# An output projection contracted in tiles of 128 rows, its last 64 rows holding high and low parts in one tile

## The chip, the cores and the metric

The kernel runs on one core of a Trainium2 chip. The metric is the device time of one execution in microseconds; before the change the median of three runs is 2657.58 (2653.82 to 2659.47). The profile is one further execution, taken by the hardware profiler. TensorE (PE) multiplies matrices and loads its stationary operand with separate instructions (PEld); VectorE (DVE), ScalarE (ACT) and GpSimd (POOL) do elementwise work; SyncE (SP) issues all DMAs from one queue.

## The reference

Input x has 2048 tokens of width 576, layer normalized without weights to xn. Attention with 32 heads of width 18 and a gated feed-forward of width 4608 both read xn, and the second gates the first:

```python
qkv = (xn @ wqkv).reshape(B, S, 3, H, Dh).transpose(2, 0, 3, 1, 4)
scores = einsum("bhqd,bhkd->bhqk", q, k) * (Dh ** -0.5)
o = einsum("bhqk,bhkd->bhqd", softmax(scores), v)
s = o.transpose(0, 2, 1, 3).reshape(B, S, D) @ wo
g = silu((gelu(xn @ w_gate) * (xn @ w_up)) @ w_down)
return x + s * g
```

The change concerns the product with wo: 2048 x 576 by 576 x 576.

## The kernel before

All large products but that of the values run in fp32r, a format of fewer bits than fp32. To keep the accuracy a factor is split into a high part, rounded to fp32r, and a low part, the rest; a product then has three terms, high by high, high by low and low by high. `split` (L93) does that on POOL with two instructions, one for each part.

The tokens are cut into four blocks of 512 (`TB`). A prologue (L138 to L349) normalizes x, computes queries, keys and values, and stores them with the split x and the split wo (`split_wo`, `store_wo`, L281 to L291; scratch `wos`) in DRAM. Then comes a row of sections, one for each 128 columns of the gate and up weights and block of tokens, 144 in all. The first nine run ahead of the attention; then 128 sections carry a quarter of a unit of attention each (a unit is four heads by one block of tokens); seven follow it. In a section TensorE does 27 pairs of gate and up products (pg and pu, L369, 64 rows each, one in the upper and one in the lower half of the array) with, between them, products for scores (pe, L684) and for their maxima (pm, L653); then the values (acc, L718, 32 products), then possibly one group of the output projection (po, L550), and in every second section the down projection (py, L406, 48 products of 128 rows and 288 columns; in the last sections 24 in each). TensorE's order is that of the program. On the other engines and in SP's queue a scheduler places instructions in the order of the times it expects, save those kept in program order.

The output projection works on `OT`, which holds the transposed attention output of a block. Each unit of attention stores its four heads, unnormalized, to DRAM (`oT`), and the reciprocals of its sums to `rT`. `load_o` (L493) brings a tile of `OT` back, and spreads the reciprocals of each head over its 18 rows (tile `den`); `norm_o` (L504) multiplies the two on POOL. A tile holds 7 heads, 126 rows (`HO`, `KO`), so that the 576 rows take four tiles of 126 and one of 72 (`NK` = 5). `load_wo` (L508) loads half the columns (288) of wo's high and low part, in two transfers each. `split_o` (L516) splits 128 tokens of all five tiles at once into `oh` and `ol`. `project_o` (L540) does one group: 128 tokens by 288 columns, 3 terms for each of 5 tiles, 15 products into one PSUM bank; eight groups a block, 32 in all.

When these happen is written in a list of due sections, `at(n, part, ...)` (L566), with three parts: 0 ahead of the values, 1 ahead of the down projection, 2 behind it. The loop at L574 fills it. A tile of `OT` is loaded when its last head is done, and normalized two sections later; the groups of a block follow in every second section of the next block. In the last block the heads of the last unit are only done at the end of the attention: its last tile is loaded right behind (L814) and normalized first thing (L801). Six of its groups then stand in the sections that follow, the last two behind all other products (L825 to L852), where VectorE combines them with the gate and SP stores the result.

Of the kernel before, what the change touches and what calls it, by code (L numbers as in the profile page):

```python
# [8 lines left out]
F32 = mybir.dt.float32  # L9
F32R = mybir.dt.float32r  # L10
AF = mybir.ActivationFunctionType
ALU = mybir.AluOpType
# [4 lines left out]
S, D, H, DH, F = 2048, 576, 32, 18, 4608  # L17
P = 128
NT = S // P
TB = 512  # L20
NB = S // TB
KT = 4
R0 = KT * P
HR = 64
# [3 lines left out]
QD = 4  # L28
VW = QD * (DH + 1)
NQ = H // QD  # L30
NU = NQ * NB
NS = 2 * NT
SLOTS = 8
NA = NS // SLOTS
# [6 lines left out]
FIRST = (0, 0, 5, 5, 6, 6, 6, 6, 6)  # L41
ATT = range(len(FIRST), len(FIRST) + NU * NA)
MROW = 3 * DH
HO = 7
KO = HO * DH
NK = -(-D // KO)
EPS = 1e-5
GC = 0.044715
GS = 0.7978845608028654
# [3 lines left out]
def f(ap):  # L53
    return ap.bitcast(F32)
# [13 lines left out]
def kernel(ctx: ExitStack, tc: tile.TileContext, x, wqkv, wo, w_gate, w_up, w_down, out):  # L68
    nc = tc.nc
    x = x.rearrange("b s d -> (b s) d")  # L70
# [9 lines left out]
    oT = dram.tile([NQ, P, S], F32, name="oT")  # L80
    wos = dram.tile([2, D, D], F32, name="wos")
# [11 lines left out]
    def split(hi, lo, raw):  # L93
        first = nc.gpsimd.tensor_scalar(hi, raw, 1.0, 1.0, op0=ALU.mult, op1=ALU.mult)  # L94
        nc.gpsimd.tensor_tensor(lo, raw, f(hi), op=ALU.subtract)  # L95
        return first
# [9 lines left out]
    def raw_tile(shape, pool=wts):  # L106
        return pool.tile(shape, F32, name="raw", tag="raw", bufs=2)
# [30 lines left out]
    with tc.tile_pool(name="pro", bufs=1) as pro, tc.tile_pool(name="pps", bufs=1, space=PSUM) as pps:  # L138
# [140 lines left out]
            nc.sync.dma_start(vs[t * P:(t + 1) * P, c * H // 2:(c + 1) * H // 2, :], v)  # L279

        def split_wo(k):  # L281
            n = min(KO, D - k * KO)
            raw = raw_tile([KO, D])
            tc.keep_in_program_order(nc.sync.dma_start(raw[0:n], wo[k * KO:k * KO + n, :]))
            hi, lo = (pro.tile([KO, D], F32R, name=f"wo{i}", tag="rawp", bufs=5) for i in range(2))
            split(hi[0:n], lo[0:n], raw[0:n])
            return k, n, hi, lo

        def store_wo(k, n, hi, lo):
            for i, t in enumerate((hi, lo)):  # L290
                tc.keep_in_program_order(nc.sync.dma_start(wos[i, k * KO:k * KO + n, :], f(t)[0:n]))  # L291

        NQT = 2 * D // P
        def after(what, before):
# [191 lines left out]


    op = ctx.enter_context(tc.tile_pool(name="op", bufs=1, reuse_waits="tile"))
    OT = op.tile([KO, NK, TB], F32, name="OT")
    nc.gpsimd.memset(OT, 0.0)  # L490
    OW, OG = {}, {}

    def load_o(b, k, pool=op):  # L493

        h0, h1 = k * HO, min(H, (k + 1) * HO)
        n = (h1 - h0) * DH
        toks = slice(b * TB, (b + 1) * TB)
        den = pool.tile([KO, TB], F32, name="den")
        nc.sync.dma_start(OT[0:n, k, :], oT.rearrange("g (a p) t -> (g a) p t", p=32)[h0:h1, 1:DH + 1, toks])
        nc.sync.dma_start(den[0:n], rT[h0:h1, toks].rearrange("h (o s) -> h o s", o=1)  # L500
                          .to_broadcast([h1 - h0, DH, TB]))
        OG["den", k] = n, den

    def norm_o(k):  # L504
        n, den = OG.pop(("den", k))
        nc.gpsimd.tensor_tensor(OT[0:n, k, :], OT[0:n, k, :], den[0:n], op=ALU.mult)

    def load_wo(c):  # L508
        for i, name in enumerate(("woh", "wol")):
            w = OW[i] = op.tile([KO, NK, 288], F32R, name=name)  # L510
            cc = slice(288 * c, 288 * c + 288)
            m = (NK - 1) * KO
            nc.sync.dma_start(f(w)[:, 0:NK - 1, :], wos[i, 0:m, cc].rearrange("(k p) n -> p k n", p=KO))
            nc.sync.dma_start(f(w)[0:D - m, NK - 1, :], wos[i, m:D, cc])

    def split_o(i, pool=op):  # L516

        j = i % (TB // P)
        oh, ol = (pool.tile([KO, NK, P], F32R, name=m) for m in ("oh", "ol"))
        split(oh, ol, OT[:, :, j * P:(j + 1) * P])  # L520
        OG["o"] = oh, ol

    def place(b, i):
# [15 lines left out]

    def project_o(b, i, S2=None, o=None):  # L540
        c, j = divmod(i, TB // P)
        cc = place(b, i)[1]
        if b < NB - 1:
            xx, yy = OG["xy"]
        po = ps.tile([P, TB], F32, name="po", tag="m", bufs=3)
        o = o or OG["o"]
        terms = [(k, x, w) for k in range(NK) for x, w in ((0, 0), (0, 1), (1, 0))]
        for m, (k, x, w) in enumerate(terms):
            n = min(KO, D - k * KO)
            nc.tensor.matmul(po[:, 0:288], o[x][0:n, k, :], OW[w][0:n, k, :], start=(m == 0), stop=(m == len(terms) - 1))  # L550
        if b < NB - 1:
            nc.vector.scalar_tensor_tensor(yy, yy, 0.25, po[:, 0:288], op0=ALU.mult, op1=ALU.mult)
            nc.gpsimd.tensor_tensor(yy, yy, xx, op=ALU.add)
            OG["y", b, i] = yy
        elif S2 is not None:
            nc.scalar.activation(S2[:, j, cc], po[:, 0:288], AF.Copy)
        return po[:, 0:288]
# [8 lines left out]
    def at(n, part, what, *args):  # L566
        todo.setdefault((n, part), []).append(lambda: what(*args))
# [3 lines left out]
            t()  # L571

    S2 = [None]
    for b in range(NB):  # L574
        last = b == NB - 1
        for k in range(NK):
            t0 = b * AB + max(-(-min(H, (k + 1) * HO) // QD) * NA + 3, 22 + 3 * k)
            if not (last and k == NK - 1):
                at(t0, 0, load_o, b, k)
                at(t0 + 2 - last, 2, norm_o, k)  # L580
        first = (b + 1) * AB + 1 if last else max((b + 1) * AB + 6, (b + 1) * NR * G - len(FIRST) + 3)
        if not last:
            first += (first + len(FIRST)) % G
        at(first - 2, 0, load_wo, 0)
        at(first - 1, 2, split_o, 0)
        for i in range(GROUPS):
            n = first + i * (1 if last else G)
            if last and n >= ENDS - 1:
                continue
            if not last:  # L590
                at(n, 0, load_xy, b, i)
                at(n + 1, 0, store_y, b, i)
            at(n, 1, lambda b=b, i=i: project_o(b, i, S2[0]))
            if i == TB // P - 1:
                at(n + 1, 0, load_wo, 1)
            if i + 1 < GROUPS:
                at(n, 2, split_o, i + 1)
# [199 lines left out]
    with tc.tile_pool(name="epi", bufs=1, reuse_waits="tile") as epi:  # L797
        S2[0] = epi.tile([P, TB // P, D], F32, name="S2")
        XX = epi.tile([P, TB // P, D], F32, name="XX")
        n = NU * NA  # L800
        todo[n, 2].insert(0, lambda: norm_o(NK - 1))  # L801
        def cut(hi, lo, raw):
            split_av(hi, lo, raw, tc.keep_in_program_order)

        def early(raw):
            wd = [epi.tile([P, G, D], F32R, name=m, bufs=2) for m in ("dh", "dl")]
            cut(*wd, raw)
            return wd

        while FF["n"] < NF:  # L810
            section([], "m" if n % 2 else "f", (lambda: raw_tile([P, G, D], epi)) if n > NU * NA + 1 else None,
                    early if n == ENDS - 1 else None)
            if n == NU * NA:
                load_o(NB - 1, NK - 1, epi)  # L814
            if n == NU * NA + 3:
                tc.keep_in_program_order(nc.sync.dma_start(XX, x[S - TB:S, :].rearrange("(j p) d -> p j d", p=P)))
            tasks(n, 0)
            downs()
            tasks(n, 1)
            tasks(n, 2)  # L820
            finish(epi, cut, 2)
            n += 1
        assert not todo
        HIND = ENDS - 1 - (NU * NA + 1)
        project_o(NB - 1, HIND, S2[0])  # L825
        os = []
        for i in range(HIND + 1, GROUPS):
            split_o(i, op if i == HIND + 1 else epi)
            os.append(OG.pop("o"))
        downs()  # L830

        def put(ss, j, cc, add):
            rows = slice(S - TB + j * P, S - TB + (j + 1) * P)
            add.tensor_tensor(ss, ss, XX[:, j, cc], op=ALU.add)
            nc.sync.dma_start(out[rows, cc], ss)

        late = {}
        for Y, j, c in finals:
            cc = slice(288 * c, 288 * c + 288)
            th = epi.tile([P, 288], F32, name="thl", bufs=len(finals))  # L840
            ss = S2[0][:, j, cc]
            gate(th, th, Y[:, j, cc])
            if c * (TB // P) + j > HIND:
                late[c * (TB // P) + j] = th, ss, j, cc
            else:
                nc.vector.scalar_tensor_tensor(ss, th, 0.25, ss, op0=ALU.mult, op1=ALU.mult)
                put(ss, j, cc, nc.gpsimd)
        for i, o in zip(range(HIND + 1, GROUPS), os):
            th, ss, j, cc = late[i]
            po = project_o(NB - 1, i, o=o)  # L850
            nc.vector.scalar_tensor_tensor(ss, th, 0.25, po, op0=ALU.mult, op1=ALU.mult)
            put(ss, j, cc, nc.vector)  # L852
# [28 lines left out]
```

## Time and profile before

| what | value |
| --- | --- |
| median of the runs | 2657.58 us |
| profiled execution, its own time | 2655.82 us |
| its span, first to last instruction | 2654.0 us |
| mean granted clock of TensorE | 0.999 |
| attention sections, first acc to last | about 308 to 2552 us |
| output projection on TensorE | 480 products, first at 988.7 us |

Time outside the span (1.8 us) is not seen by the profile. Durations of products overlap: one is put down with 0.29 us though the next starts 0.13 us later, so the distance of the starts is what a product costs. A shape such as 72*128 is the active rows and columns of the array.

### The profile page before, as it was taken

Reading aid. Unit: us, or ns where it says so; the run is one execution under the profiler, and the core shown is the slowest. Engines: PE = TensorE matmul, PEld = TensorE weight load, DVE = VectorE, ACT = ScalarE, POOL = GpSimd, SP = SyncE. Lnnn points to the kernel's source line nnn. Section 1 sums busy time; section 2 is a strip of 40 time slices with the busy share of each in tenths; the row PEclk is TensorE's granted clock in tenths of the full one; section 3 lists DMA queues with packets and bytes.
Section 4 is the critical chain, followed back from the end, with each engine's and each line's share of the span. In section 5 each row is a group of like instructions: output and inputs, shape, how many; then the busy total and the mean of one; then the engine's idle time right before and its main releaser. Section 6 shows DMA issues by size and latency. Waiting matters only on the chain.

```text
span 2654.0 us, 55993 instructions
## 1 busy us (share of the span) xinstructions
PE 2639.6 (99%) x21032; PEld 2052.3 (77%) x21032; DVE 2002.5 (75%) x3440; ACT 1504.2 (57%) x2690; POOL 1392.5 (52%) x1488
## 2 busy tenths in 40 slices
PE   9999999999999999999999999999999999999999
PEld 8888777777777777777777777777777777777788
DVE  5327888888887888777888887778888877788445
ACT  3222466666666666555666665556666655566632
POOL 2126544545466555555447655554446755555564
PEclk9999999999999999999999999999999999999999
DMA  8875433333345434444336434434335444444341
GB/s 257 265 240 144 115 99 101 98 101 104 98 124 133 106 100 108 121 113 124 100 109 156 117 103 105 124 96 136 104 103 122 133 115 123 107 109 122 77 110 58
DMA packets 390874, 323.66 MB, mean 122 GB/s; under 512 B 105736, under 2 KB 305928, under 8 KB 390604
## 3 DMA queue, kind: packets, MB, share of 16 engines
q1 hardware_dynamic: 390604, 320.08, 44.6%
q8 instruction: 167, 2.74, 0.5%
q14 instruction: 103, 0.84, 0.1%
HBM read 266.58 MB, written 52.85 MB: 120 GB/s over the span
## 4 chain that ended last, share of the span: by engine, by line
PE 97%; POOL 1%; DVE 1%; DMA 1%; issue 0%; ACT 0%; SPq 0%; POOLq 0%; DVEq 0%
PE pg L369 26%; PE py L406 18%; PE acc L718 17%; PE pe L684 10%; PE pm L653 9%; PE pu L369 8%; PE po L159 7%; PE po L550 2%; PE pt L221 0%; POOL wl L95 0%; DVE mx L654 0%; DMA xx<-in_A_x_dram 0%; POOL th L432 0%; PE pm L667 0%; DMA raw<-in_B_w_gate_dram 0%
## 5 line engine op out<-in xcount | busy, mean ns | idle before, releaser
L685 ACT ACTIVATE pT<-pe 128x512 f32<-128x512 f32 x2048 | 1162.8, 599 | 704.1 <-PE pm L653 476.1
L654 DVE TENSOR_REDUCE mx<-pm 128x1 f32<-128x512 f32 x2048 | 1288.5, 685 | 52.1 <-PE pm L653 28.0
L369 PE MATMUL pg<-xd,wh 64*128 64x512 f32 x2592 | 948.3, 398 | 0.5 <-issue 0.5
L369 PE MATMUL pu<-xd,wh 64*128 64x512 f32 x2592 | 948.3, 398 | 0.0
L684 PE MATMUL pe<-q,KS 56*128 56x512 f32 x2048 | 812.5, 405 | 0.0
L653 PE MATMUL pm<-KS,q 54*128 54x512 f32 x2048 | 794.6, 394 | 4.7 <-DVE mx L654 4.7
L369 PEld LDWEIGHTS pg<-xd,wh 64*128 64x128 f32 x2592 | 483.0, 187 | 66.0 <-issue 34.8
L94 POOL TENSOR_SCALAR wh<-raw 128x384 fp32r<-128x384 f32 x432 | 223.8, 519 | 547.6 <-PE pu L369 292.7
L369 PE MATMUL pg<-xd,wl 64*128 64x512 f32 x1296 | 508.2, 392 | 0.0
L369 PE MATMUL pu<-xd,wl 64*128 64x512 f32 x1296 | 507.8, 392 | 0.0
L369 PEld LDWEIGHTS pu<-xd,wh 64*128 64x128 f32 x2592 | 484.1, 187 | 7.6 <-DVE t L387 1.6
L718 PE MATMUL acc<-pT,VS 128*32 128x512 f32 x4096 | 466.0, 595 | 0.0
L95 POOL TENSOR_TENSOR wl<-raw,wh 128x384 fp32r<-128x384 f32 x432 | 442.3, 1025 | 34.3
L684 PEld LDWEIGHTS pe<-q,KS 56*128 56x128 f32 x2048 | 370.2, 184 | 81.3 <-ACT pT L685 20.2
L653 PEld LDWEIGHTS pm<-KS,q 54*128 54x128 f32 x2048 | 377.0, 185 | 29.2 <-DVE mx L654 7.6
L412 DVE TENSOR_TENSOR Y<-py,Y 128x288 f32<-128x288 f32 x544 | 248.7, 457 | 187.6 <-PE py L406 186.7
L406 PE MATMUL py<-dh,hh 128*128 128x288 f32 x1152 | 352.8, 306 | 1.4 <-DVE Y L410 1.2
L406 PE MATMUL py<-dl,hh 128*128 128x288 f32 x1152 | 339.6, 295 | 0.0
L406 PE MATMUL py<-dh,hl 128*128 128x288 f32 x1152 | 338.7, 294 | 0.0
L718 PEld LDWEIGHTS acc<-pT,VS 128*32 128x32 f32 x4096 | 120.6, 109 | 275.7 <-issue 264.4
L369 PEld LDWEIGHTS pg<-xd,wl 64*128 64x128 f32 x1296 | 242.4, 187 | 17.0
L406 PEld LDWEIGHTS py<-dh,hh 128*128 128x128 f32 x1152 | 215.8, 187 | 44.1 <-issue 37.7
(118 smaller groups left out, 2935.2 us busy)
## 6 DMA issues: line engine op xcount, KB each, us to landing
KS<-qk SPq DMA_DIRECT2D x1536, 36.0 KB
raw<-in_B_w_gate_dram SPq DMA_DIRECT2D x144, 288.0 KB
raw<-in_B_w_up_dram SPq DMA_DIRECT2D x144, 288.0 KB
raw<-in_B_w_down_dram SPq DMA_DIRECT2D x68, 576.0 KB
VS<-vs SPq DMA_DIRECT2D x128, 152.0 KB
qk<-t SPq DMA_DIRECT2D x72, 256.0 KB
q<-qk SPq DMA_DIRECT2D x384, 36.0 KB
xd<-xhs SPq DMA_DIRECT2D x24, 384.0 KB
```

The lines of the kernel that those rows point to most:

```text
L94: first = nc.gpsimd.tensor_scalar(hi, raw, 1.0, 1.0, op0=ALU.mult, op1=ALU.mult)
L95: nc.gpsimd.tensor_tensor(lo, raw, f(hi), op=ALU.subtract)
L159: nc.tensor.matmul(o, st, m, start=(i == 0), stop=(i == len(TERMS) - 1))
L369: nc.tensor.matmul(o, w[1 + wp][k][rr, c, :], xd[xp][k][rr, c, :], start=(i == 0), stop=(i == len(terms) - 1))
L406: nc.tensor.matmul(py, a[:, tt], w[:, g, cc], start=(n == 0), stop=(n == 3 * G - 1))
L412: nc.vector.tensor_tensor(yy, py, yy, op=ALU.add)
L550: nc.tensor.matmul(po[:, 0:288], o[x][0:n, k, :], OW[w][0:n, k, :], start=(m == 0), stop=(m == len(terms) - 1))
L653: nc.tensor.matmul(pm, QS[u, r][rr, t * P:(t + 1) * P], KS[(u * NA + c) % KB][r][rr, :], start=True, stop=True)
L654: nc.vector.tensor_reduce(MX[u][:, 2 * r + a, t, c:c + 1], pm, axis=AX.X, op=ALU.max)
L684: nc.tensor.matmul(pe, KS[(u * NA + c) % KB][r][rr, t * P:(t + 1) * P], QS[u, r][rr, :], start=True, stop=True)
L685: nc.scalar.activation(PT[u, kt][:, 2 * r + a, :], pe, AF.Exp, scale=SCALE)
L718: nc.tensor.matmul(ACC[u][32 * a:32 * a + 32, :], VS[(u * NA + c) % VB][:, v:v + 32], pt[:, a, :], start=(kt == 0), stop=(kt == NT - 1), s ...
```

## The change

The rows of the attention output are cut at multiples of 128 and no longer between heads: four tiles of 128 rows and one of 64 (`NK` is `KT` + 1, again 5). In the last tile rows 64 to 127 of `oh`, zero after the split, receive a copy of the low parts (`split_o`, on POOL), and rows 64 to 127 of the high part of wo a second copy of its last 64 rows (`load_wo`, one more transfer). One product of 128 rows then gives high by high and low by high together, and one of 64 rows high by low; a group has 14 products.

A tile now begins and ends inside a head, so `load_o` transfers its parts one by one: the rest of a head, the whole heads, the start of a head; two transfers for each, 26 a block. The fourth tile (rows 384 to 511) now reaches into head 28, which belongs to the last unit, so it is loaded four sections later, together with the fifth, and in the last block in two parts (`LATE`): the heads that are done ahead, the last one behind the attention. Both last tiles are normalized then.

```diff
-HO = 7
-KO = HO * DH
-NK = -(-D // KO)
+NK = KT + 1
...
-    def load_o(b, k, pool=op):
-
-        h0, h1 = k * HO, min(H, (k + 1) * HO)
-        n = (h1 - h0) * DH
-        toks = slice(b * TB, (b + 1) * TB)
-        den = pool.tile([KO, TB], F32, name="den")
-        nc.sync.dma_start(OT[0:n, k, :], oT.rearrange("g (a p) t -> (g a) p t", p=32)[h0:h1, 1:DH + 1, toks])
-        nc.sync.dma_start(den[0:n], rT[h0:h1, toks].rearrange("h (o s) -> h o s", o=1)
-                          .to_broadcast([h1 - h0, DH, TB]))
-        OG["den", k] = n, den
+    def load_o(b, k, pool=op, heads=range(H)):
+
+        toks = slice(b * TB, (b + 1) * TB)
+        if ("den", k) not in OG:
+            OG["den", k] = pool.tile([P, TB], F32, name="den")
+        den = OG["den", k]
+        row, end = k * P, min(D, (k + 1) * P)
+        while row < end:
+            h, d = divmod(row, DH)
+            m = max(1, (end - row) // DH) if d == 0 else 1
+            e = min(DH, d + end - row)
+            n = m * (e - d)
+            rows = slice(row - k * P, row - k * P + n)
+            row += n
+            if h in heads:
+                nc.sync.dma_start(OT[rows, k, :], oT.rearrange("g (a p) t -> (g a) p t", p=32)[h:h + m, 1 + d:1 + e, toks])
+                nc.sync.dma_start(den[rows], rT[h:h + m, toks].rearrange("h (o s) -> h o s", o=1)
+                                  .to_broadcast([m, e - d, TB]))
...
     def load_wo(c):
         for i, name in enumerate(("woh", "wol")):
-            w = OW[i] = op.tile([KO, NK, 288], F32R, name=name)
+            w = OW[i] = op.tile([P, NK, 288], F32R, name=name)
             cc = slice(288 * c, 288 * c + 288)
-            m = (NK - 1) * KO
-            nc.sync.dma_start(f(w)[:, 0:NK - 1, :], wos[i, 0:m, cc].rearrange("(k p) n -> p k n", p=KO))
-            nc.sync.dma_start(f(w)[0:D - m, NK - 1, :], wos[i, m:D, cc])
+            nc.sync.dma_start(f(w)[:, 0:KT, :], wos[i, 0:R0, cc].rearrange("(k p) n -> p k n", p=P))
+            for a in range(2 - i):
+                nc.sync.dma_start(f(w)[HR * a:HR * a + HR, KT, :], wos[i, R0:D, cc])
 
     def split_o(i, pool=op):
 
         j = i % (TB // P)
-        oh, ol = (pool.tile([KO, NK, P], F32R, name=m) for m in ("oh", "ol"))
+        oh, ol = (pool.tile([P, NK, P], F32R, name=m) for m in ("oh", "ol"))
         split(oh, ol, OT[:, :, j * P:(j + 1) * P])
+        nc.gpsimd.tensor_copy(oh[HR:P, KT, :], ol[0:HR, KT, :])
         OG["o"] = oh, ol
...
-        terms = [(k, x, w) for k in range(NK) for x, w in ((0, 0), (0, 1), (1, 0))]
-        for m, (k, x, w) in enumerate(terms):
-            n = min(KO, D - k * KO)
+        terms = [(k, x, w, P) for k in range(KT) for x, w in ((0, 0), (0, 1), (1, 0))] + [(KT, 0, 0, P), (KT, 0, 1, HR)]
+        for m, (k, x, w, n) in enumerate(terms):
             nc.tensor.matmul(po[:, 0:288], o[x][0:n, k, :], OW[w][0:n, k, :], start=(m == 0), stop=(m == len(terms) - 1))
...
+    LATE = range(H - QD), range(H - QD, H)
     for b in range(NB):
         last = b == NB - 1
         for k in range(NK):
-            t0 = b * AB + max(-(-min(H, (k + 1) * HO) // QD) * NA + 3, 22 + 3 * k)
-            if not (last and k == NK - 1):
+            t0 = b * AB + max(-(-min(D, (k + 1) * P) // (QD * DH)) * NA + 3, 22 + 3 * k)
+            if last and k == KT - 1:
+                at(NU * NA - 1, 0, load_o, b, k, op, LATE[0])
+            if not last or k < KT - 1:
+                t0 += k == KT
                 at(t0, 0, load_o, b, k)
-                at(t0 + 2 - last, 2, norm_o, k)
+                at(*((t0 + 2 - last, 2) if k < KT - 1 else (t0 + 1, 0)), norm_o, k)
...
-        todo[n, 2].insert(0, lambda: norm_o(NK - 1))
+        for k in (KT, KT - 1):
+            todo[n, 2].insert(0, lambda k=k: norm_o(k))
...
             if n == NU * NA:
-                load_o(NB - 1, NK - 1, epi)
+                load_o(NB - 1, KT - 1, op, LATE[1])
+                load_o(NB - 1, KT, epi)
```

The prologue's `split_wo` and `store_wo` cut wo in the same way, 128 rows instead of 126.

More of the change, by code (lines that the diff above doesn't have):

```diff
@@ L281, in split_wo @@
         def split_wo(k):
-            n = min(KO, D - k * KO)
-            raw = raw_tile([KO, D])
-            tc.keep_in_program_order(nc.sync.dma_start(raw[0:n], wo[k * KO:k * KO + n, :]))
-            hi, lo = (pro.tile([KO, D], F32R, name=f"wo{i}", tag="rawp", bufs=5) for i in range(2))
+            n = min(P, D - k * P)
+            raw = raw_tile([P, D])
+            tc.keep_in_program_order(nc.sync.dma_start(raw[0:n], wo[k * P:k * P + n, :]))
+            hi, lo = (pro.tile([P, D], F32R, name=f"wo{i}", tag="rawp", bufs=5) for i in range(2))
             split(hi[0:n], lo[0:n], raw[0:n])
@@ L290, in store_wo @@
             for i, t in enumerate((hi, lo)):
-                tc.keep_in_program_order(nc.sync.dma_start(wos[i, k * KO:k * KO + n, :], f(t)[0:n]))
+                tc.keep_in_program_order(nc.sync.dma_start(wos[i, k * P:k * P + n, :], f(t)[0:n]))
         NQT = 2 * D // P
@@ L488 @@
     op = ctx.enter_context(tc.tile_pool(name="op", bufs=1, reuse_waits="tile"))
-    OT = op.tile([KO, NK, TB], F32, name="OT")
+    OT = op.tile([P, NK, TB], F32, name="OT")
     nc.gpsimd.memset(OT, 0.0)
     OW, OG = {}, {}
-    def load_o(b, k, pool=op):
-        h0, h1 = k * HO, min(H, (k + 1) * HO)
-        n = (h1 - h0) * DH
+    def load_o(b, k, pool=op, heads=range(H)):
         toks = slice(b * TB, (b + 1) * TB)
-        den = pool.tile([KO, TB], F32, name="den")
-        nc.sync.dma_start(OT[0:n, k, :], oT.rearrange("g (a p) t -> (g a) p t", p=32)[h0:h1, 1:DH + 1, toks])
-        nc.sync.dma_start(den[0:n], rT[h0:h1, toks].rearrange("h (o s) -> h o s", o=1)
-                          .to_broadcast([h1 - h0, DH, TB]))
-        OG["den", k] = n, den
+        if ("den", k) not in OG:
[13 more added lines that the diff above has]
+                                  .to_broadcast([m, e - d, TB]))
@@ L504, in norm_o @@
     def norm_o(k):
-        n, den = OG.pop(("den", k))
-        nc.gpsimd.tensor_tensor(OT[0:n, k, :], OT[0:n, k, :], den[0:n], op=ALU.mult)
+        n = min(P, D - k * P)
+        nc.gpsimd.tensor_tensor(OT[0:n, k, :], OT[0:n, k, :], OG.pop(("den", k))[0:n], op=ALU.mult)
     def load_wo(c):
         for i, name in enumerate(("woh", "wol")):
-            w = OW[i] = op.tile([KO, NK, 288], F32R, name=name)
+            w = OW[i] = op.tile([P, NK, 288], F32R, name=name)
             cc = slice(288 * c, 288 * c + 288)
-            m = (NK - 1) * KO
-            nc.sync.dma_start(f(w)[:, 0:NK - 1, :], wos[i, 0:m, cc].rearrange("(k p) n -> p k n", p=KO))
-            nc.sync.dma_start(f(w)[0:D - m, NK - 1, :], wos[i, m:D, cc])
+            nc.sync.dma_start(f(w)[:, 0:KT, :], wos[i, 0:R0, cc].rearrange("(k p) n -> p k n", p=P))
+            for a in range(2 - i):
+                nc.sync.dma_start(f(w)[HR * a:HR * a + HR, KT, :], wos[i, R0:D, cc])
@@ L546, in project_o @@
         o = o or OG["o"]
-        terms = [(k, x, w) for k in range(NK) for x, w in ((0, 0), (0, 1), (1, 0))]
-        for m, (k, x, w) in enumerate(terms):
-            n = min(KO, D - k * KO)
+        terms = [(k, x, w, P) for k in range(KT) for x, w in ((0, 0), (0, 1), (1, 0))] + [(KT, 0, 0, P), (KT, 0, 1, HR)]
+        for m, (k, x, w, n) in enumerate(terms):
             nc.tensor.matmul(po[:, 0:288], o[x][0:n, k, :], OW[w][0:n, k, :], start=(m == 0), stop=(m == len(terms) - 1))
```

## The prediction

> **What bounds the kernel now.** I read the page's busy shares and its chain first, then the chain in order of time around the output projection, and then the timeline of TensorE at the ends of its groups of products. From the page:
>
> ```profile
> PE 2639.6 (99%) x21032; PEld 2052.3 (77%) x21032; DVE 2002.5 (75%) x3440; ACT 1504.2 (57%) x2690; POOL 1392.5 (52%) x1488
> PE 97%; POOL 1%; DVE 1%; DMA 1%; issue 0%; ACT 0%; SPq 0%; POOLq 0%; DVEq 0%
> ```
>
> TensorE is busy for 99% of the span and makes 97% of the chain that ended last; the other engines idle for a quarter to a half of it. So a change is worth what it does to TensorE's own stream, unless it delays something that TensorE reads. The chain in order of time:
>
> ```profile
> 1523.90 6.62 PE py L406 x48
> 1555.03 3.57 PE acc L718 x32
> 1560.78 6.45 PE py L406 x48
> ```
>
> The columns are start, length, work. In the second case a projection group (po, 15 products) stands between acc and py, from 1558.60 to 1560.78. Behind acc the 48 py products take 6.62 us, behind po 6.45. So something of 0.17 us is paid once, by whichever group follows acc. The timeline of TensorE (start, duration, then the product with its rows*columns) says what it is:
>
> ```profile
> 1558.53 0.40 PE L550 MATMUL po<-woh,oh 126*128 126x288 f32 x1
> 1558.77 0.29 PE L550 MATMUL po<-wol,oh 126*128 126x288 f32 x1
> ...
> 1560.35 0.30 PE L550 MATMUL po<-wol,oh 72*128 72x288 f32 x1
> 1560.49 0.29 PE L550 MATMUL po<-woh,ol 72*128 72x288 f32 x1
> 1560.62 0.29 PE L406 MATMUL py<-dh,hh 128*128 128x288 f32 x1
> ```
>
> Durations overlap, so price by the distance of starts. From 1558.77 to 1560.62 are 14 products: 0.132 us each, whether of 126 rows or 72, and py follows po at the same distance. Only the first po stands 0.24 ahead of its successor. Two more boundaries, from 128-row work to the 64-row pairs of gate and up, and back:
>
> ```profile
> 2600.69 0.29 PE L550 MATMUL po<-woh,ol 72*128 72x288 f32 x1
> 2600.92 0.49 PE L369 MATMUL pg<-xd,wh 64*128 64x512 f32 x1
> 2601.25 0.39 PE L369 MATMUL pg<-xd,wl 64*128 64x512 f32 x1
> 2601.48 0.39 PE L369 MATMUL pg<-xd,wh 64*128 64x512 f32 x1
> ...
> 2606.95 0.39 PE L369 MATMUL pu<-xd,wh 64*128 64x512 f32 x1
> 2607.26 0.40 PE L406 MATMUL py<-dh,hh 128*128 128x288 f32 x1
> 2607.50 0.29 PE L406 MATMUL py<-dl,hh 128*128 128x288 f32 x1
> 2607.63 0.29 PE L406 MATMUL py<-dh,hl 128*128 128x288 f32 x1
> ```
>
> Into 64 rows: the first pg comes 0.23 after the last po instead of 0.13, and the next pg 0.33 later instead of 0.23: 0.20 us. Back to 128 rows: py comes 0.31 after the last pair instead of 0.23, and the second py 0.24 later instead of 0.13: 0.19 us. Each change between 64-row and 128-row products so costs about 0.195 us, half before its first product and half behind it.
>
> **The change part by part.**
>
> *One product less.* 32 groups (four blocks of 512 tokens, eight groups each) go from 15 products to 14: 32 x 0.132 = 4.2 us less.
>
> *The last product has 64 rows.* Its terms are (KT, 0, 0, 128) and (KT, 0, 1, 64). The built program puts a product of 72 rows in a 128x128 tile of the array and one of 64 rows in a 64x128 tile, the form of pg and pu. So every group now ends with a change to 64-row form. What follows it, by the built order (the same as before):
> - 24 groups in the attention sections, and one late group, are followed by py or by another 128-row group: two changes that were not there, 2 x 0.195 = 0.39, less the product saved, 0.13: +0.26 us each. 25 x 0.26 = +6.5 us.
> - 5 groups of the last block are followed by pg. The change there exists already (2600.69 to 2600.92) and only moves one product ahead: -0.13 each, -0.65 us.
> - the last two groups, back to back at the end: three new changes, 0.585, less two products, 0.265: TensorE ends 0.32 later. VectorE covers this: it works without a gap from 2638.9 on, reads the last po at 2650.06, and that po ends at 2648.3; 1.7 us of cover. Without it, +0.3.
>
> *Price of a change, bounded.* The lowest row is the small product of the maxima (128*32) ahead of py:
>
> ```profile
> 762.27 0.25 PE L667 MATMUL pm<-identr,m 128*32 128x128 f32 x1
> 762.35 0.35 PE L406 MATMUL py<-dh,hh 128*128 128x288 f32 x1
> 762.54 0.29 PE L406 MATMUL py<-dl,hh 128*128 128x288 f32 x1
> ```
>
> py follows at 0.08 and its successor 0.19 later, 0.06 over 0.13. So a change of form may cost as little as 0.06. At 0.06 the 25 groups give 25 x (0.12 - 0.13) = -0.3 and all -0.9 us; at 0.20, the dearest row, +6.05. I take 0.195, since those rows switch between just these two forms, at full 128 columns.
> The Trainium skill ("TensorEngine Tiling (Array Packing)", Tiling Modes, Key Properties) says that changing the tiling mode, and not only the tile, drains TensorE. The rows of 128 and 64 rows agree; the row of 128*32 ahead of py, with 0.06 to 0.14, hardly does. By the rule, which has no figure, the sum keeps its sign.
>
> *POOL.* Each of 32 splits gains a copy of 64x128 (the low part into rows 64 to 127 of oh). Nearest rows: the 128x128 cast of the identity, 0.289 us, and the 64x1536 copies of xd, 1.466, which scaled to 128 columns give 0.12. I take 0.29: 9.3 us of POOL. It is hidden: the split after the group at 1558.53 ends at 1563.2, its products start at 1595. The normalizations keep their number (20) and width. That of tile 3 moves from section 33 of a block to 36, that of tile 4 stays in 37 but ahead of its downs; where the lead of hh and hl over their py is least (1.2 to 2.4 us, at the three changes of block) POOL's built order sets no further wait ahead of them, and the weight splits queued behind run far ahead (1555.72 plus 1.01 for a section that starts at 1581.09). Cover gone, each microsecond late would be one on TensorE.
>
> *SP and DMA.* load_o goes from 10 to 26 transfers per block, load_wo from 4 to 5 per half: 64 + 8 more issues at 0.33 to 0.85 us, some 50 us of SP's 2654, spread over four blocks. Behind them wait keys, values and raw weights; the keys are asked for seven chunks ahead and the weights as above, so I cost this at nothing. The five tiles of wo in the prologue keep their number of instructions and grow by two rows. If a raw weight came too late, it would be the 0.6 us of each issue ahead of it, about 2 us at a time.
>
> *The last block*, where the lead is short. Three reciprocal transfers instead of one after 2560.61: the last is issued 1.3 us later, and the raw weights behind it too. The first normalization starts at 2564.71 as before; the second adds 1.3 and two copies 0.6: POOL is 2.0 us late. Its next weight splits end at 2575.0; TensorE needs the first at 2577.04 and the second two microseconds on. Cover 2.0 to 4, just enough: 0, at the dear end +1.
>
> Sum: 6.5 - 0.65 = +5.9 us. The profiled execution took 2655.82 (span 2654.0), which becomes 2661.7; the median of the three runs is 1.76 above it, so 2657.58 + 5.9 = 2663.5.
>
> **The rivals.**
> - *The change of form is free or nearly so for a lone product* (the other side). For it: the 0.06 at 762.54, and that pg and pu, priced above, come in pairs. Against it: both directions cost 0.19 or more, whenever they occur. It decides from 0.066 us per change, where two cost as much as the product saved. At zero: -4.2, so 2653.4; at 0.06, 2656.7.
> - *Only one of the two changes is paid*, since the other's weight load hides in the short product's drain: 25 x (0.195 - 0.13) - 0.65 = +1.0, so 2658.6. For it: half of the price lies behind the first product. Against: the load of py's weights starts only with py, at 2607.26, though it had time.
> - *A late transfer or POOL takes TensorE down as well*: section at 2577 with 2.0 us of cover against 2.0 used, and three blocks where reciprocals come in three pieces and POOL waits for the last (78.1 us of such waits before, none of which TensorE saw). One such stall per block of 0.5 to 1 us: +2 to +4, so 2666.5.
>
> **How the numbers follow.** Forecast 0.66, free change 0.11, one change paid 0.09, extra stall 0.14. What a measurement here can tell from no change is about 0.2%, 5.3 us; three runs spread over 5.7. The forecast, at +5.9 (0.22%), lies just past that bound; two thirds and a little more of its chance fall beyond (0.47), the rest within (0.19). The stall adds 0.14 to slower, and what of the one-change case comes out dearer 0.03 more; the free and the one-change case give 0.12 to the same and 0.05 to faster. Slower 0.64, same 0.31, faster 0.05. Range 2658.5 to 2667.5: from the one-change case to the stall; out of it lies the free change and what little is dearer than the stall.
>
> **What would show it.** In the changed kernel's timeline: the last po at 64*128, about 0.23 behind the one before; the next py 0.33 behind it and 0.24 ahead of its second; py runs of 6.6 us behind po, not 6.45; a group with its py 0.26 longer. Wrong would be: starts that stay 0.13 apart around the 64-row product; idle time of TensorE ended by POOL or by a DMA near 2577; a VectorE gap ahead of line 851's successor at the end.

## The result and the profile after

The changed kernel takes 2662.11 us, the median of 16 runs (2659.51 to 2663.86); the kernel before, run beside it, takes 2657.30 (16 runs, 2653.82 to 2659.47). The ratio is 1.0018, with an interval of 1.0011 to 1.0025: 4.8 us slower, where +5.9 was forecast. The same comparison, made once more on another occasion, gave 2663.76 against 2658.70, +5.1 us and a ratio of 1.0021 (1.0012 to 1.0030). Both intervals hold the forecast ratio of 1.0022. The 4.8 us are less than the 5.3 us that the prediction took for the least that can be told from no change; with sixteen runs of each kernel the interval leaves out no change all the same.

The profiled execution took 2662.27 us, with a span of 2660.5 against 2654.0. Its page gives the busy time of each engine, and the engines' shares of the chain that ended last:

```profile
PE 2645.4 (99%) x21000; PEld 2053.6 (77%) x21000; DVE 2002.6 (75%) x3440; ACT 1506.9 (57%) x2690; POOL 1402.4 (53%) x1520
...
PE 97%; POOL 1%; DVE 1%; issue 0%; ACT 0%; DMA 0%; POOLq 0%; DVEq 0%
```

TensorE has 32 products less and is busy 5.8 us longer; its share of the chain is the same. So the time went into TensorE's own stream. The chain in order of time (start, duration, work) around two sections with a down projection, the second of them with a projection group ahead of it:

```profile
1527.71 6.62 PE py L404 x48
...
1558.87 3.57 PE acc L728 x32
1562.44 2.23 PE po L556 x14
1564.67 6.63 PE py L404 x48
```

Behind a group the 48 py products now take 6.63 us, as they do behind acc, and not the 6.45 of before. The group itself takes 2.23 us for 14 products, where it took 2.18 (1558.60 to 1560.78) for 15. TensorE's timeline at the end of this group (start, duration, and the active rows*columns):

```profile
1563.92 0.29 PE L556 MATMUL po<-woh,ol 128*128 128x288 f32 x1
1564.05 0.29 PE L556 MATMUL po<-woh,oh 128*128 128x288 f32 x1
1564.28 0.39 PE L556 MATMUL po<-wol,oh 64*128 64x288 f32 x1
1564.60 0.40 PE L404 MATMUL py<-dh,hh 128*128 128x288 f32 x1
1564.84 0.29 PE L404 MATMUL py<-dl,hh 128*128 128x288 f32 x1
1564.97 0.29 PE L404 MATMUL py<-dh,hl 128*128 128x288 f32 x1
```

Here the three distances are seen that carry the result: 0.23 into the 64-row product, 0.32 out of it, and 0.24 from the first py to the second, where 128-row products follow each other at 0.13. Over all 25 such places the medians are 0.225, 0.324 and 0.237 us. Less 3 x 0.132 that is 0.39 us for the two changes of form, less one product saved 0.26.

In the late groups, where pg and pu follow, the same timeline shows the other case:

```profile
2607.27 0.29 PE L556 MATMUL po<-woh,oh 128*128 128x288 f32 x1
2607.49 0.40 PE L556 MATMUL po<-wol,oh 64*128 64x288 f32 x1
2607.49 0.50 PE L367 MATMUL pu<-xd,wh 64*128 64x512 f32 x1
2607.73 0.39 PE L367 MATMUL pg<-xd,wh 64*128 64x512 f32 x1
...
2613.94 0.40 PE L404 MATMUL py<-dh,hh 128*128 128x288 f32 x1
```

The change into 64-row form (0.22) is paid once, ahead of the lone product, and pu starts together with it. The lone product is not free even so: pg, which in the kernel before starts beside pu, comes 0.24 later here. From the last 128-row product to py it is 6.67 us (2607.27 to 2613.94), against 6.57 before (from the last po at 2600.69 to 2607.26): 0.10 us for the lone product, where one of 128 rows takes 0.13. The five places agree within 0.01 us.

### The profile page after: what moved, and what is told of

The parts are those of the page before. It is cut to its first block, busy times and chain, and to the rows that moved or that the text cites. A ratio compares the mean times of both kernels' runs of the same rounds, so it can differ in the third digit from the quotient of the medians.

```text
span 2660.5 us, 56058 instructions
## 1 busy us (share of the span) xinstructions
PE 2645.4 (99%) x21000; PEld 2053.6 (77%) x21000; DVE 2002.6 (75%) x3440; ACT 1506.9 (57%) x2690; POOL 1402.4 (53%) x1520
## 4 chain that ended last, share of the span: by engine, by line
PE 97%; POOL 1%; DVE 1%; issue 0%; ACT 0%; DMA 0%; POOLq 0%; DVEq 0%
PE pg L367 26%; PE py L404 18%; PE acc L728 17%; PE pe L694 10%; PE pm L663 9%; PE pu L367 8%; PE po L157 7%; PE po L556 2%; PE po L210 0%; PE pt L219 0%; POOL wl L93 0%; DVE mx L664 0%; PE pm L677 0%; POOL th L430 0%; POOL wh L92 0%
```

## The experiments

**Where the form is paid: all products with 128 rows.** The lone product is padded: the low part of wo's last 64 rows is loaded a second time into rows 64 to 127 of its tile, and the last product reads all 128 rows. It so adds low by low, a term that the kernel before leaves out.

```diff
-            for a in range(2 - i):
+            for a in range(2):
...
-  ... + [(KT, 0, 0, P), (KT, 0, 1, HR)]
+  ... + [(KT, 0, 0, P), (KT, 0, 1, P)]
```

> The changed kernel with its last product over 128 rows: rows 64 to 127 of the low part of wo receive a second copy of its last 64 rows too (one more transfer in each load_wo), so that the product adds a term low by low, and no product of the group has 64 rows. The theory that the changes of form between 128-row and 64-row products cost the time (0.195 us each), and that transfers and copies are hidden: 14 products at 0.132 and no change of form, against the kernel before 30 x 0.132 = 4.0 us faster (2 of the 32 groups stand behind VectorE at the end), ratio 0.9985. The rival that the copies, transfers and later normalizations cost the time: as the changed kernel, about 4.8 us slower than before, ratio 1.0018.

Measured: 2651.70 us (11 runs, 2650.59 to 2654.39) against 2657.10 for the kernel before; ratio 0.9978 (0.9969 to 0.9987). That is 5.4 us faster than the kernel before and about 10 faster than the change as it was made, by giving one product 64 rows more. The end of the same group in its timeline:

```profile
1560.76 0.29 PE L556 MATMUL po<-woh,oh 128*128 128x288 f32 x1
1560.89 0.30 PE L556 MATMUL po<-wol,oh 128*128 128x288 f32 x1
1561.04 0.29 PE L404 MATMUL py<-dh,hh 128*128 128x288 f32 x1
1561.16 0.29 PE L404 MATMUL py<-dl,hh 128*128 128x288 f32 x1
```

All starts are 0.12 to 0.15 apart. The saved product is now a gain, and the whole loss hung on the form of the last one.

**Fifteen products again, with the new tiles and loads.** To the kernel with full rows a fifteenth product of 128 rows is added (low by low of the last tile once more), so that TensorE does what it did before, and only the loads, POOL's copies and the moved normalizations are new.

```diff
-  ... + [(KT, 0, 0, P), (KT, 0, 1, P)]
+  ... + [(KT, 0, 0, P), (KT, 0, 1, P), (KT, 1, 1, P)]
```

> As the kernel with the last product over 128 rows, with a fifteenth product of 128 rows added (low by low once more, in the size of fp32's last bits). It has the 15 products and the forms of the kernel before, and all transfers, copies and normalizations of the changed one. Theory of the form: the time of before, within 1 us, ratio 1.000. Rival of the transfers and copies: these cost about 4.8 + 4.2 = 9 us, which the product saved hides in part in the changed kernel; here they show whole, ratio 1.0034.

Measured: 2655.61 us (11 runs, 2652.92 to 2659.07), ratio 0.9995 (0.9987 to 1.0004). The transfers and POOL cost nothing that can be seen.

**The 64-row product first.** In the first three blocks the lone product is moved from the end of the group to its beginning, behind acc, which has a form of its own (128*32).

```diff
+        if b < NB - 1:
+            terms = terms[-1:] + terms[:-1]
```

> The changed kernel with the 64-row product first in its group, in the 24 groups of the attention sections; the last block as in the changed kernel. There a change of form stands at the start of the group already, behind acc, so one change is added and not two. Theory of the form: 24 x (0.195 - 0.132) = +1.5, the one late group +0.26, five late groups -0.65, together 1.1 us slower than before, ratio 1.0004; in the trace the first po 0.32 ahead of the second, and py 0.13 behind the last po. If two changes are paid wherever the product stands, or if transfers cost the time: 4.8 us slower, as the changed kernel.

Measured: 2656.10 us (11 runs, 2653.62 to 2658.32), ratio 0.9996 (0.9988 to 1.0005). The same work in another order takes back the loss: behind acc a group pays for a change whatever its first product is, so that one of the two is left.

```profile
1559.86 0.40 PE L558 MATMUL po<-wol,oh 64*128 64x288 f32 x1
1560.18 0.40 PE L558 MATMUL po<-woh,oh 128*128 128x288 f32 x1
1560.42 0.29 PE L558 MATMUL po<-wol,oh 128*128 128x288 f32 x1
1560.54 0.29 PE L558 MATMUL po<-woh,ol 128*128 128x288 f32 x1
```

**The form change alone, in the kernel before.** The last product of each group reads 64 rows and not 72; loads, tiles and the number of products stay. It leaves out 8 rows of one low product.

```diff
-            n = min(KO, D - k * KO)
+            n = min(KO, D - k * KO) if m < len(terms) - 1 else HR
```

> The kernel before, with the last of the 15 products of each group cut from 72 rows to 64; it leaves out the low part of 8 of 576 rows. Nothing else differs: no transfer, no copy, no count of products. Theory of the form: two changes more in 25 groups, 25 x 0.39 = 9.75 us slower than before, ratio 1.0037; the five late groups ahead of pg unchanged. Rival that a lone 64-row product costs no more than one of 72: no difference, ratio 1.0000; that only one of the two changes is paid: 4.9 us, 1.0018.

Measured: 2667.00 us (5 runs, 2665.24 to 2668.93), ratio 1.0036 (1.0023 to 1.0048), +9.9 us. Reading fewer rows makes the kernel slower by twice what the whole change does. Its timeline, at the same place:

```profile
1567.26 0.29 PE L550 MATMUL po<-wol,oh 72*128 72x288 f32 x1
1567.48 0.40 PE L550 MATMUL po<-woh,ol 64*128 64x288 f32 x1
1567.81 0.40 PE L406 MATMUL py<-dh,hh 128*128 128x288 f32 x1
1568.04 0.29 PE L406 MATMUL py<-dl,hh 128*128 128x288 f32 x1
```

**What the kernel before loses elsewhere.** These four fit the price of the form, but the three with the new loads came out 1.4 to 2.1 us below what was expected of them, and the changed kernel 1.1 below the forecast. A look for something that the kernel before pays and the others not gave this: in sections that end a unit of attention, two VectorE operations of 16 columns on the negated maxima (m), of 0.17 us each, at times take up to 1.0 us, and a pu product then waits about 0.4 us. The profile of before had 8 such waits of over 0.2 us in its attention sections, that of after 1. One of them, from a second profile of the changed kernel (all engines; in square brackets the idle time ahead and what ended it):

```profile
1618.10 1.00 POOL L93 TENSOR_TENSOR wl<-raw,wh 128x384 fp32r<-128x384 f32 x1
1618.14 0.99 DVE L672 TENSOR_TENSOR m<-nm,m 128x16 fp32r<-128x16 f32 x1
1619.06 0.68 DVE L381 SCALAR_TENSOR_TENSOR t<-t,pg 128x512 f32<-128x512 f32 x1
...
1620.39 0.69 DVE L385 TENSOR_TENSOR t<-t,pu 128x512 f32<-128x512 f32 x1 [0.66 <-ACT t L384]
...
1620.72 0.50 PE L367 MATMUL pg<-xd,wh 64*128 64x512 f32 x1
1621.13 0.18 PEld L367 LDWEIGHTS pu<-xd,wh 64*128 64x128 f32 x1 [0.23 <-DVE t L385]
```

The small operation starts 0.04 us after POOL's and ends with it. VectorE so reads the pu of the section 0.8 us late, and the pu of the next, which needs that bank, comes 0.42 us after its pg instead of beside it. The Trainium skill ("SBUF — State Buffer", SBUF: two separate sides) says that GpSimd and VectorE share a pair of ports, which goes for a whole instruction to whichever starts first, where VectorE works in a mode of two ports, or has two inputs in SBUF and GpSimd reads SBUF too. These rows, a subtraction with two inputs on each engine, agree.

So the two operations were moved to ScalarE, in the kernel before, in the changed kernel and in the one with full rows. The low part becomes zero, which shifts the scores by a slightly different value that the softmax divides out.

```diff
-            nc.vector.tensor_copy(m2[:, 0], nm)
-            nc.vector.tensor_tensor(m2[:, 1], nm, f(m2)[:, 0], op=ALU.subtract)
+            nc.scalar.activation(m2[:, 0], nm, AF.Copy)
+            nc.scalar.activation(m2[:, 1], nm, AF.Copy, scale=0.0)
```

> The kernel before, with the two small operations on the negated maxima (m: the high part, and its remainder) moved from VectorE to ScalarE; the remainder is set to zero, so the score is shifted by the high part alone (the softmax divides the same shift out again). TensorE's order is unchanged. In the profile of the kernel before, these operations take up to 1.0 us instead of 0.17 where a POOL instruction on the weights (wl or wh) is running, VectorE reads pu that much later, and the next pu product waits about 0.4 us, in 8 sections: 3.2 us in all. Theory A (those waits are lost time of the kernel before, which the new arrangement mostly escapes): the waits go, about -3 us, 2654.3, ratio 0.9988; no pu wait over 0.3 us in a section of maxima. Rival B (they are an accident of the one profiled execution, or are not what separates the forecast from the result): 2657.3, ratio 1.0000.

> The changed kernel with the same two operations moved to ScalarE. Theory A: the changed kernel's profile shows only 0.5 us of these waits, so it gains 0.5 us at most: 2661.6, ratio 1.0016; and its distance to the run before this one (the kernel before with the same move) becomes the full price of the form changes, +5.9 to +7 us instead of the +4.8 between the two kernels as they are. Rival B: 1.0018, and the distance to the run before stays at +4.8 or less.

> All fourteen products of a group with 128 rows (the lone 64-row product padded by the low half and zero rows of wo, as in the run with full rows), and the two small operations on ScalarE. Sum of the parts, theory A: from 2651.7 another -0.4 us: 2651.3, ratio 0.9977, 3 us faster than the kernel before with the same move (15 products less one, 4.2 us less). Rival B: 2651.7, ratio 0.9978.

> The kernel before once more, for a second profile. Theory A (the collisions belong to the order of the work): again 6 to 10 pu waits of about 0.4 us in the sections of maxima, mostly the same ones. Rival B (an accident of one execution): another number and other sections.

(The third text calls the padding rows of wo zero; they hold its low part, as said above.) Measured, beside 2656.73 us for the kernel before:

| kernel | median us (runs) | ratio, interval | pu waits over 0.2 us |
| --- | --- | --- | --- |
| before, maxima on ScalarE | 2655.15 (11) | 0.9993, 0.9984 to 1.0002 | 0 |
| changed, maxima on ScalarE | 2659.70 (11) | 1.0011, 1.0002 to 1.0020 | 0 |
| full rows, maxima on ScalarE | 2649.88 (8) | 0.9972, 0.9961 to 0.9982 | 0 |
| before, second look | 2656.57 (1) | none | 2 |

The first of them is 1.6 us below the kernel before, between theory A's 3 and rival B's nothing, and its interval still holds no change. The second came out below both texts (1.0011 for 1.0016 or 1.0018). The third is 5.3 us below the first, where its text expects 3.

In the first run, the operations on all 32 units (duration in ns: least, median, greatest):

```profile
L661 ACT ACTIVATE m<-nm x32: 215/216/218, 281.9 to 2473.8; 128x16 fp32r<-128x16 f32 x32
L662 ACT ACTIVATE m<-nm x32: 198/200/202, 282.0 to 2473.9; 128x16 fp32r<-128x16 f32 x32
```

On ScalarE they take the same time in every unit, and the waits are gone. But theory A, as an account of the missing microsecond, falls. The second profile of before has 2 waits and not 8, and the second profile of the changed kernel 7: they come and go from execution to execution in both arrangements. Hundredths of a microsecond decide it: in the four profiles with these operations on VectorE, the 69 subtractions that began between 0.02 us ahead of a wl instruction of POOL and 0.004 behind its start took 0.17 to 0.18 us, and the 18 that began 0.03 to 0.20 behind it took 0.86 to 1.01, until 0.03 after its end. And the distance from the changed kernel to the kernel before, both without the waits, is 4.55 us; it did not widen. The waits are real (5 on average over the two profiles of before, 0.4 us each, 2 us), and not what separates the forecast from the result.

**Do the new loads gain something?** What was left is that the new arrangement itself might give a microsecond. The kernel with fifteen full products got the move to ScalarE too, and ran beside the kernel before with the same move, whose products are the same, and beside the changed kernel once more.

> Fifteen products of 128 rows in the new tiles, with the new loads, copies and order of normalizations, and the small operations on the maxima on ScalarE. TensorE's products are those of the kernel before with the same move, which runs beside it, so the difference of the two is what the new loads and POOL's copies do and nothing else. Theory C (the new arrangement itself gives about 1 us, the difference between the forecast and the result): 1 to 1.5 us below the kernel before with the move. Rival D (that difference is scatter): the same time as the kernel before with the move, within 0.5 us.

> The kernel before with the small operations on ScalarE once more, beside the run with fifteen full products. From the first time: 1.6 us below the kernel before, ratio 0.9994; the gap to it a steady gain of the move if it comes again.

> The changed kernel as it is, once more. Theory C: again about +4.8 us, ratio 1.0018. Rival D: nearer to the forecast of +5.9, ratio 1.0022.

Measured, beside 2658.70 us for the kernel before: fifteen full products 2655.49 (11 runs; 0.9987, 0.9978 to 0.9996), the kernel before with the move 2654.95 (11 runs; 0.9985, 0.9976 to 0.9994), the changed kernel 2663.76 (10 runs; 1.0021, 1.0012 to 1.0030). The first two differ by 0.5 us, and in the other direction, as rival D has it. The changed kernel's +5.1, though, is nearer to theory C's +4.8 than to +5.9. And of all comparisons of the new arrangement with the old, with the maxima on the same engine in both, this is the only one above the price of the forms: the other seven are 0.8 to 2.1 us below it (some share a partner). The profiles show no such gain: in the two with the move that reach the first down product at the same time (225.92 us before, 225.89 changed), the spans are 2651.9 and 2657.9, 6.0 apart. Nor is a microsecond much beside what separates two executions of one kernel: the changed kernel reaches its first down product at 225.77 us in one profile and at 223.09 in the other. So the difference between +5.9 and +4.8 is of the size of the scatter, and a gain of about a microsecond from the new arrangement is neither shown nor excluded. The move to ScalarE gave 3.7 us here and 1.6 before, so a gain of some 2 to 3 us.

**The price of a group, read from the traces.** With the waits gone, two traces can be laid over each other product by product. This is the time that each of the 24 groups in the attention sections adds, from acc ahead of it to the section behind it (ns, against the kernel before with the maxima on ScalarE; the last line against the later profile of that same kernel):

```
kernel                                forecast   mean   least  greatest
changed, maxima on ScalarE                 260    257     239       277
full rows, maxima on ScalarE              -132   -132    -154      -115
64-row product first                       ~60     62      32        86
kernel before, last product 64 rows        390    383     351       424
fifteen full products, on ScalarE            0      2     -15        21
```

The traces of the third and fourth line have one and two waits left somewhere, but the mean is little moved by them. (The forecast of the third line is 0.195 for one change less 0.132.) In this view the mean price of a group can be judged to some 0.01 us, far finer than by the medians, whose intervals are some 2 us to either side.

## Why the prediction was right

*The price of a change of form* was taken as 0.195 us, from places where pg and pu stand next to 128-row products, and applied to a lone product. It was 0.195, half of 0.257 + 0.132: the 24 groups cost 0.257 each, 6.17 us in all, against 24 x 0.26. The row with 0.06, which had set the lower bound, belongs to another pair of forms. The rival of a free change (2653.4) and the one with a single change paid (2658.6) fall by the timeline, and by the run in the kernel before: +9.9 us, where one change in each group would have given about half.

*The late groups and the end.* From the start of the last section ahead of these groups to the last down product the trace of the changed kernel with the move is 0.40 us shorter than that of the kernel before with it (78.54 us against 78.94); the forecast was -0.65 + 0.26 = -0.39. In the profiles without the move each of the five groups ahead of a pair takes, from its first product to the third py behind it, 8.64 us on average against 8.79: 0.15 less, where the forecast had 0.13. At the end three changes were to be covered by VectorE, with 1.7 - 0.3 = 1.4 us to spare. The timeline of the changed kernel:

```profile
2654.81 0.39 PE L556 MATMUL po<-wol,oh 64*128 64x288 f32 x1
```

```profile
2655.95 0.79 DVE L846 TENSOR_TENSOR S<-S,XX 128x288 f32<-128x288 f32 x1
2656.66 0.44 DVE L863 SCALAR_TENSOR_TENSOR S<-thl,po 128x288 f32<-128x288 f32 x1
```

The last po ends at 2655.20, and VectorE reads it at 2656.66 without having waited: 1.46 us.

*POOL and the last block.* The copies take 0.285 us (median of 32) where 0.29 was taken. The critical place was the weight split behind the two normalizations, where POOL was to be 2.0 us late against a cover of 2.0 to 4. POOL's timeline of the changed kernel, and the first products of the section that read the weights' high and low part:

```profile
2573.40 1.70 POOL L512 TENSOR_TENSOR OT<-OT,den 64x512 f32<-64x512 f32 x1 [2.26 <-DMA den<-rT]
...
2580.71 0.52 POOL L527 CAST oh<-ol 64x128 fp32r<-64x128 f32 x2
2581.32 0.98 POOL L92 TENSOR_SCALAR wh<-raw 128x384 fp32r<-128x384 f32 x2
2582.27 1.99 POOL L93 TENSOR_TENSOR wl<-raw,wh 128x384 fp32r<-128x384 f32 x2
```

```profile
2583.85 0.50 PE L367 MATMUL pu<-xd,wh 64*128 64x512 f32 x1
...
2584.19 0.40 PE L367 MATMUL pu<-xd,wl 64*128 64x512 f32 x1
```

In the kernel before these weight splits began at 2572.05, here at 2581.32, 9.27 later; TensorE's section begins 6.81 later (2577.04 to 2583.85). So POOL lost 2.5 us against TensorE, more than the 2.0 taken. But the cover was larger as well. The prediction set the end of the second wl (2575.0) against the start of the section; the first wl, which is needed first, was ready at 2574.03 and read at 2577.37, 3.35 us later. Here the first of the two is ready at 2583.29 and read at 2584.19: 0.9 us are left, and 0.54 in the trace with the move. The cover held, by a narrow margin and with both of its terms taken too small, and the rival of an extra stall there (2666.5) did not come true. SP's 72 more issues and the loads in pieces cost nothing that can be seen, as the runs with fifteen full products show.

*What was not seen.* At the changes of block the prediction looked at the lead of hh and hl over their py, 1.2 to 2.4 us, and at POOL. There py waits in both kernels, and for VectorE, which adds an earlier py to Y. The waits of TensorE between 790 and 840 us and between 2065 and 2125 us (total, count, longest) in the kernel before:

```profile
PE py L406 <- DVE Y L410: 0.9, 1, 0.9
...
PE py L406 <- DVE Y L410: 0.3, 1, 0.3
```

and in the changed kernel, where only the second place has one:

```profile
PE py L404 <- DVE Y L408: 0.6, 1, 0.6
```

These waits differ between executions (0 to 1.7 us each over the profiles). They are a term that the sum lacked; in this pair it is -0.6 us. Over the three changes of block they add up to 1.3 us on average in the five profiles with the old loads (0.7 to 2.4) and to 1.1 in the eight with the new ones (0.3 to 1.7), so that little of the term is left. What makes them longer or shorter was not tried.

So the terms of the sum have the sizes that the traces show, and the mechanism is the one forecast. What was too large by 1.1 us is the total against the medians; that is within their intervals, and whether a small gain of the new arrangement has a part in it stays open.

## What to carry to other kernels

A product of 64 rows alone among 128-row products costs more than the full one: count the changes of form that an edit makes, at about 0.2 us each in this kernel, before counting the products that it saves. Pad the lone product to 128 rows (here 0.9978 in place of 1.0018), or, if it must stay short, put it next to work that changes the form anyway. And the price of an edit at one place, where it is near the scatter of the medians, is read more finely by laying two traces over each other, place by place, than from the medians.

## What the runs showed that was not expected

- The lone 64-row product and the pu that follows it in the late groups start within 0.01 us of each other (both at 2607.49): the two use different halves of the rows and run beside each other. The pg of that pair comes a step later instead, and the lone product costs 0.10 us there, against 0.52 between 128-row products (0.39 for two changes of form and 0.13 for itself).
- A VectorE operation on 16 columns takes 0.17 us, or up to 1.0 when it starts inside a POOL instruction that splits the weights, since it then ends only with that one; the one with two inputs and the plain copy are both hit (0.174 at the least, 0.895 for the copy and 0.993 for the subtraction at the most, in the second profile of the changed kernel). Whether it is hit turns on a start 0.03 us earlier or later. On ScalarE it is 0.20 to 0.22 in all profiles with the move. Together with the full rows the move gives the fastest version, 2649.88 us, 0.9972 (0.9961 to 0.9982) of the kernel before.
